# Joined loads of two head pairs, other row orders for k and v, and q turned by the crossbar for all later pairs

## The chip, the cores and the metric

The kernel runs on one core of one Trainium2 chip. The metric is the device time of one execution in microseconds (us). Engines: TensorE (PE in the profile, its weight loads PEld), VectorE (DVE), ScalarE (ACT), GpSimd (POOL) and SyncE (SP, which here only issues DMAs). Inputs are in DRAM, the output goes back there; SBUF holds 128 partitions, and TensorE writes into PSUM.

## The reference

Eight batches of eight heads, 576 rows, 64 columns a head; then a two-layer network over all 4608 rows. All in float32.

```python
scores = scale * np.matmul(q, k.transpose(0, 1, 3, 2))
thresh = np.max(scores, axis=-1, keepdims=True) - tau          # tau = 0.02
scores = np.where(scores >= thresh, scores, -1000000000.0)
scores = scores - np.max(scores, axis=-1, keepdims=True)
attn = np.exp(scores)
attn = attn / (np.sum(attn, axis=-1, keepdims=True) + 1e-09)
attn_out = np.matmul(attn, v)                                  # (8, 8, 576, 64)
x = attn_out.transpose(0, 2, 1, 3).reshape(4608, 512)
h = x @ w_in                                                   # (512, 2048)
out = (h - np.tanh(h)) @ w_out                                 # (2048, 512)
```

## The kernel before, in words

**Tiles.** The 64 heads are taken as 32 pairs, four to a batch. A pair has 2 x 576 query rows, that is nine tiles of 128 rows: four of each head, and one shared tile with the last 64 rows of both (`place`, L307). The main loop (L730) goes through 288 tiles, one a step. For one tile the work is spread over many steps: scores are made 8 steps ahead (`scores`, L313), TensorE's result is copied out by DVE, which also takes the maximum (L346); 5 steps ahead ScalarE makes z from it (`kink`, L365, L373); at its own step the exponential is taken (`weights`, L382); two steps later TensorE multiplies by v (`attend`, L414). z has to be turned between kink and weights. For pairs 0 to 5 TensorE does that; from pair 6 on, SP issues one crossbar transpose (a DMA from SBUF to SBUF) for every two tiles, `zT` (L380), and ScalarE reads zT in the exponential (L409).

**q, k and v of a pair.** `load` (L138) brings each as float32: rows 0 to 511 of both heads with four rows to a partition (L145), and the last 64 rows of both heads in a second, small DMA (L153 for q and k, where partition 2s + h takes row s of head h; L151 for v, into 64 partitions). `split` (L186) makes q and k on POOL into two fp16 parts, high and low, stored side by side. `turn` (L253) transposes them so that the 128 partitions hold 64 high and 64 low parts: on TensorE with nine transposes into PSUM (L240) and a DVE copy out (L268), or, for q of some pairs, by a crossbar transpose that SP issues (L257, `qT`). For k a copy `kS` with both halves swapped follows on POOL (L274). `split_v` (L219) copies v to bf16 on POOL. `q_by_dma` (L249) names the pairs whose q goes by the crossbar: from pair 8 on those with p % 4 != 0.

A score tile is four matmuls (L336): q against kT and against kS, each over 512 and then 64 keys. The shared tile (L327) does that for each head in one half of the array; where q was turned by the crossbar its rows alternate by head, so the weights are read with step two.

**The network.** TensorE makes h (`hidden`, L505, PSUM banks `psH`, two of them), ScalarE the tanh (L518), DVE the difference g (L524), TensorE the output (`project`, L531), DVE or ScalarE copy it out and SP stores it (L547). These steps are put between the attention's by a written pattern (L563).

**What sets the order.** Everything is issued in program order, on each engine's own in-order queue. A plan (L671 to L699) says at which step each part of a pair's preparation is issued, counted back from `first = 9 p - 8`. For the later pairs: loads of k, q, v at first - 17, - 15, - 13 for even pairs and - 16, - 14, - 12 for odd ones; splits at - 10 and - 9 (at - 8 and - 7 where TensorE turns q), k turned at - 6, v split at - 4, q turned by the crossbar at - 7 (even) or - 6 (odd), by TensorE at - 2. Within a step the order is: scores, kink and zT, tanh, weights, network, stores, attend, then the plan. So on SP a step's zT comes before the stores and loads of that step. Weights of the network come in 16 pieces during the first 54 steps (L663, L667).

Of the kernel before, what the change touches and what calls it, by code (L numbers as in the profile page):

```python
# [9 lines left out]
F32 = mybir.dt.float32  # L10
BF16 = mybir.dt.bfloat16
FP16 = mybir.dt.float16
# [6 lines left out]
def kernel(  # L19
# [11 lines left out]
    nc = tc.nc  # L31
    P = 128
# [13 lines left out]
    HPAIR = H // 2  # L46
# [85 lines left out]


    raws = {}

    def load(p, t):  # L138
        b, h0 = p // HPAIR, 2 * (p % HPAIR)
        hs = slice(h0, h0 + 2)  # L140
        src = {"k": k, "q": q, "v": v}[t]
        eng = nc.sync
        r = raws[p, t] = raw_pool.tile([P, 10, D], F32, name=f"{t}raw", tag=t)
        n = 8 if t == "v" else 10
        eng.dma_start(  # L145
            out=r[:, 0:n, :].rearrange("p (h c) d -> p h (c d)", h=2)[:, :, 0 : 4 * D],
            in_=src[b, hs, 0:512, :].rearrange("h (p c) d -> p h (c d)", c=4),
        )
        rem = src[b, hs, 512:S, :].rearrange("h s d -> s h d")
        if t == "v":  # L150
            eng.dma_start(out=r[0:64, 8:10, :], in_=rem)  # L151
        else:
            eng.dma_start(out=r[:, 4, :], in_=rem)  # L153

    def load_first(t, h, eng):

        src = {"k": k, "q": q}[t]
        if (0, t) not in raws:
            raws[0, t] = raw_pool.tile([P, 10, D], F32, name=f"{t}raw", tag=t)
        r = raws[0, t]  # L160
        if h is None:
            rem = src[0, 0:2, 512:S, :].rearrange("h s d -> s h d")
            eng.dma_start(out=r[:, 4, :], in_=rem)
        else:
            eng.dma_start(
                out=r[:, 5 * h : 5 * h + 4, :].rearrange("p c d -> p (c d)"),
                in_=src[0, h, 0:512, :].rearrange("(p c) d -> p (c d)", c=4),
            )
# [17 lines left out]
    def split(p, t):  # L186
        x = raws.pop((p, t))[:, 0:9, :]
        hl = hl_pool.tile([P, TPP, 2, D], FP16, name=f"{t}hl", tag=t)
        nc.gpsimd.tensor_scalar(
            out=x, in0=x, scalar1=QKSC, scalar2=1.0, op0=ALU.mult, op1=ALU.mult  # L190
        )
        nc.gpsimd.tensor_copy(out=hl[:, :, 0, :], in_=x)
        nc.gpsimd.tensor_tensor(  # L193
            out=hl[:, :, 1, :], in0=x, in1=hl[:, :, 0, :], op=ALU.subtract
        )
        hls[p, t] = hl
# [21 lines left out]

    def split_v(p):  # L219
        r, vb = raws.pop((p, "v")), vbs[p % NV]  # L220
        nc.gpsimd.tensor_copy(
            out=vb[:, :, 0:4, 0:D],
            in_=r[:, 0:8, :].rearrange("p (h c) d -> p h c d", h=2),
        )
        nc.gpsimd.tensor_copy(out=vb[0:64, :, 4, 0:D], in_=r[0:64, 8:10, :])
        nc.gpsimd.tensor_copy(out=vb[64:P, :, 5, 0:D], in_=r[0:64, 8:10, :])

    mats = {}  # L230


    by_head = lambda ap: ap.rearrange("p (s h) -> p h s", h=2)
    in_heads = lambda ap: ap.rearrange("p (h s) -> p h s", h=2)

    def turn_chunk(out, c, lhsT):
        rhs = ident_f16
        if c == 4:
            out, rhs = in_heads(out), by_head(rhs)
        nc.tensor.matmul(  # L240
            out=out, lhsT=lhsT, rhs=rhs, is_transpose=True, start=True, stop=True
        )
# [5 lines left out]

    def q_by_dma(p):  # L249

        return p >= 2 * HPAIR and p % 4 != 0

    def turn(p, t):  # L253
        hl = hls.pop((p, t))
        if t == "q" and q_by_dma(p):
            m = mats[p, t] = qk_pool.tile([P, W], FP16, name=f"{t}T", tag=t)
            nc.sync.dma_start_transpose(  # L257
                out=m.rearrange("p (c r) -> p c r", c=TPP),
                in_=hl.rearrange("p c a d -> p (c a d)"),
            )  # L260
            return
        ps = ps_big.tile([P, W], FP16, name=f"ps_{t}", tag="big")
        for c in range(TPP):
            turn_chunk(
                ps[:, c * P : (c + 1) * P], c, hl[:, c, :, :].rearrange("p a d -> p (a d)")
            )
        m = qk_pool.tile([P, W], FP16, name=f"{t}T", tag=t)
        nc.vector.tensor_copy(out=m, in_=ps)  # L268
        mats[p, t] = m
        if t == "k":  # L270
            sw = qk_pool.tile([P, W], FP16, name="kS", tag="ks")
            for lo, hi in ((0, D), (D, 0)):
                o, i = sw[lo : lo + D, :], m[hi : hi + D, :]
                nc.gpsimd.tensor_copy(out=o, in_=i)  # L274
            mats[p, "ks"] = sw

    def turn_first(t, part):

        hl = hls[0, t[0]]
        c0, c1 = ((0, 5), (5, TPP))[part]  # L280
        pl, tag = (ps_y, "y") if t == "ks" else (ps_h, "h")
        ps = pl.tile([P, 5 * P], FP16, name=f"ps1_{t}", tag=tag)
        for c in range(c0, c1):
            o = ps[:, (c - c0) * P : (c - c0 + 1) * P]
            if t == "ks":
                for a in range(2):
                    turn_chunk(o[64 * a : 64 * a + 64, :], c, hl[:, c, 1 - a, :])
            else:
                turn_chunk(o, c, hl[:, c, :, :].rearrange("p a d -> p (a d)"))
        if part == 0:  # L290
            mats[0, t] = qk_pool.tile([P, W], FP16, name=f"{t}T", tag=t)
        dst, n = mats[0, t][:, c0 * P : c1 * P], (c1 - c0) * P
        if part == 1 or t == "q":
            nc.scalar.copy(out=dst, in_=ps[:, 0:n])
        else:
            nc.vector.tensor_copy(out=dst, in_=ps[:, 0:n])


    MAIN = (slice(0, 512), slice(640, W))
    REM = (slice(512, 576), slice(576, 640))  # L300
    scs, mxs, nbs, zs, zts, pts, ops = {}, {}, {}, {}, {}, {}, {}

    def kind(i):
# [9 lines left out]
    def scores(i):  # L313
        p, hh, t = place(i)
        qT, kT, kS = mats[p, "q"], mats[p, "k"], mats[p, "ks"]
        ps = ps_big.tile([P, 1024], F32, name="psS", tag="big")
        main, rem, lo = slice(0, 512), slice(512, 576), 0
        if kind(i) == "B":
            main, rem, lo = slice(512, 1024), slice(448, 512), 448
        if hh is None:  # L320
            qrem = REM
            if q_by_dma(p):
                qrem = (slice(512, 640, 2), slice(513, 640, 2))
            for n, kk in enumerate((kT, kS)):
                for dst, srcs in ((main, MAIN), (rem, REM)):
                    for hh in range(2):
                        nc.tensor.matmul(  # L327
                            out=ps[64 * hh : 64 * hh + 64, dst],
                            lhsT=qT[:, qrem[hh]], rhs=kk[:, srcs[hh]],
                            start=(n == 0), stop=(n == 1),  # L330
                        )
        else:
            lhs = qT[:, (5 * hh + t) * P : (5 * hh + t + 1) * P]
            for n, kk in enumerate((kT, kS)):
                for dst, src in ((main, MAIN[hh]), (rem, REM[hh])):
                    nc.tensor.matmul(  # L336
                        out=ps[:, dst], lhsT=lhs, rhs=kk[:, src],
                        start=(n == 0), stop=(n == 1),
                    )
        sc = sc_pool.tile([P, S], F32, name="sc")  # L340
        if kind(i) == "B":
            mx = mxs[i] = mxs.pop(i - 1)
        else:
            mx = mxs[i] = mx3[i // 2 % len(mx3)]
        c = int(kind(i) == "B")
        nc.vector.tensor_scalar(  # L346
            out=sc, in0=ps[:, lo : lo + S], scalar1=SC, scalar2=None,
            op0=ALU.mult, op1=ALU.max, accum_out=mx[:, c : c + 1],
        )
        scs[i] = sc  # L350
# [163 lines left out]
    def bend():  # L514
        while halves:
            m, n, ps = halves.pop(0)
            th = t_pool.tile([P, MB], F32, name="th")
            nc.scalar.activation(out=th, in_=ps, func=ACT.Tanh)  # L518
            ths.append((m, n, ps, th))

# [8 lines left out]
    def project(m, ms, part, ps, last, cols=slice(0, d_model)):  # L529
# [4 lines left out]
            )  # L534
        if part == 3:
            nc_ = cols.stop - cols.start
            yo = y_pool.tile(
                [P, nc_], F32, name="yo", tag="yo" if nc_ == d_model else f"yo{int(last)}",
                bufs=2 if nc_ == d_model else 1,
            )  # L540
            if last:
                nc.scalar.copy(out=yo, in_=ps)
            else:
# [16 lines left out]
    EARLY = lambda m: 3 if m else 3  # L560
    LAST = 1

    PATTERN = lambda m: '-h--h-hh--h-hh-h-hh-h--hh-h--hh-y-yy' if m == 0 else 'hyhyhyhyhyhyhyhyhyhyhyhyhyhyhyhy' if m == B - 2 else 'yhyhyyy-yhyhhyyhy-hhhyhh-hyhyhy-yhhy'  # L563

    FIRST = 3
    quarters = lambda m: [(m, ms, part) for ms in range(4) for part in range(4)]
# [112 lines left out]
    )  # L679

    plan = {}
    for p in range(1, NPAIR):
        first = TPP * p - AHEAD
        for d, f in PREP[3 if p == 1 else 0 :]:
            d -= p == 1 and d == 3
# [150 lines left out]
```

## Time and profile before

| | |
|---|---|
| runs (us) | 518.08, 518.08, 518.48; median 518.08 |
| profiled execution: time, span | 518.02 us, 516.2 us |
| granted TensorE clock | 1.0 |
| busy share of the span: PE, PEld, DVE, ACT, POOL | 96%, 55%, 81%, 84%, 56% |
| DMA: bytes moved, read from and written to HBM | 86.79 MB, 36.70 MB, 9.44 MB |
| zT transposes, qT transposes issued by SP | 117, 18 |
| main loads of k, q, v (256 KB each) issued by SP | 31, 31, 32 |
| remainders of k, q, v (32 KB each) issued by SP | 31, 32, 32 |
| TensorE transposes of q (L240), copies of q by DVE (L268) | 126, 13 |

The profile is of one execution. A line of a timeline gives the start and the length in us, the engine and line, the operation, what it writes and reads, and in brackets how long the engine was idle before it and what ended that. `SPq` lines are SP's queue: the time for which the instruction held SP, not that of the transfer. A landing time counts from the start of the issue to the last byte's semaphore. "x4" on a line is several instructions shown as one, with the stretch that they cover.

### The profile page before, as it was taken

To read this page: it belongs to the slowest core of one execution; us is meant where nothing else is said; L and a number is where in the kernel's file an instruction comes from. 1 tells how busy PE (TensorE), PEld (TensorE's weight loads), DVE (VectorE), ACT (ScalarE), POOL (GpSimd) and SP (SyncE) were. 2 spreads that over 40 slices of the span, in tenths; PEclk is the share of its full clock that TensorE was granted. 3 is DMA by queue.
4 is the path that set the end of the run, shared out by engine and by line. 5 is a ranking of instruction groups with operands and counts; after the bars stand their busy time and mean duration, and the time that the engine had idled before them with its cause. 6 is when DMAs were issued, how large, how long until landed. Compare 5 with 4: busy or idle time off the path is not lost.

```text
span 516.2 us, 12626 instructions
## 1 busy us (share of the span) xinstructions
PE 497.8 (96%) x4540; PEld 285.3 (55%) x4606; DVE 418.8 (81%) x1179; ACT 432.8 (84%) x617; POOL 290.2 (56%) x390
## 2 busy tenths in 40 slices
PE   8999899889999999999999999999999999999997
PEld 4666566555555555555555555555555555544444
DVE  5999889998899988998899888998999887644440
ACT  5999999999899989998999989998999899543430
POOL 8999999776565656566666656566656620000000
PEclk9999999999999999999999999999999999999999
DMA  7852659999999999999999998999989976311013
GB/s 205 259 151 90 205 196 227 165 190 181 193 190 190 207 203 194 187 193 212 201 176 190 197 220 195 183 198 197 203 179 193 172 140 116 97 41 42 20 43 82
DMA packets 208607, 86.79 MB, mean 168 GB/s; under 512 B 176160, under 2 KB 200992, under 8 KB 208544
## 3 DMA queue, kind: packets, MB, share of 16 engines
q1 hardware_dynamic: 207952, 85.56, 80.6%
q8 instruction: 36, 0.59, 0.5%
q10 hardware_dynamic: 592, 0.43, 0.3%
q14 instruction: 27, 0.22, 0.1%
HBM read 36.70 MB, written 9.44 MB: 89 GB/s over the span
## 4 chain that ended last, share of the span: by engine, by line
PE 77%; POOL 9%; ACT 4%; DVE 3%; issue 3%; DMA 2%; SPq 1%; POOLq 0%; ACTq 0%; DVEq 0%
PE psY L531 22%; PE psH L505 19%; PE psS L336 18%; PE psO L439 5%; PE psS L327 3%; PE psHt L505 3%; PE ps_k L240 3%; POOL kS L274 2%; DMA kraw<-in_k_dram 2%; POOL w_in_sb L655 1%; PE psO L450 1%; ACT pT L409 1%; POOL khl L193 1%; PE psO L432 1%; ACT z L373 1%
## 5 line engine op out<-in xcount | busy, mean ns | idle before, releaser
L373 ACT ACTIVATE z<-sc,nb 128x576 bf16<-128x576 f32 x288 | 217.5, 770 | 23.9 <-DVE nb L358 22.2
L346 DVE TENSOR_SCALAR_CACHE_REDUCE sc<-psS 128x576 f32<-128x576 f32 x288 | 213.7, 752 | 17.5 <-PE psS L336 13.3
L531 PE MATMUL psY<-w_out_sb,g 128*128 128x512 bf16 (+1 forms) x565 | 140.2, 373 | 1.3 <-issue 0.2
L409 ACT ACTIVATE pT<-zT 128x1152 f16<-128x1152 bf16 x117 | 134.8, 1152 | 1.7 <-DMA zT<-z 1.4
L274 POOL COPY kS<-kT 64x1152 f16<-64x1152 f16 x62 | 70.7, 1141 | 110.9 <-DVE nb L358 59.6
L505 PE MATMUL psH<-xT,w_in_sb 128*128 128x512 bf16 x443 | 117.8, 379 | 3.5 <-issue 1.1
L336 PE MATMUL psS<-kT,qT 128*128 128x512 f16 (+1 forms) x512 | 104.4, 285 | 4.7 <-DVE sc L346 2.4
L336 PEld LDWEIGHTS <-qT 128*128 128x128 f16 x1024 | 72.9, 97 | 56.5 <-issue 5.5
L524 DVE SCALAR_TENSOR_TENSOR g<-th,psH 128x512 bf16<-128x512 f32 x128 | 87.5, 683 | 18.3 <-ACT th L518 18.0
L336 PE MATMUL psS<-kS,qT 128*128 128x512 f16 x496 | 101.4, 286 | 0.0
L518 ACT ACTIVATE th<-psH 128x512 f32<-128x512 f32 x128 | 74.5, 582 | 20.9 <-PE psH L505 20.9
L531 PEld LDWEIGHTS <-g 128*128 128x128 bf16 x592 | 51.1, 98 | 54.0 <-DVE g L524 0.4
L505 PEld LDWEIGHTS <-w_in_sb 128*128 128x128 bf16 x576 | 49.0, 98 | 56.3 <-issue 3.4
L439 PE MATMUL psO<-vb,pT 128*128 128x65 bf16 x1024 | 53.3, 194 | 0.0
L439 PEld LDWEIGHTS <-pT 128*128 128x128 f16 x1024 | 44.2, 98 | 9.4
L193 POOL TENSOR_TENSOR khl<-kraw,khl 128x576 f16<-128x576 f32 x31 | 39.7, 1280 | 2.6
L193 POOL TENSOR_TENSOR qhl<-qraw,qhl 128x576 f16<-128x576 f32 x31 | 39.7, 1280 | 2.6
L401 ACT ACTIVATE pT<-psZ 128x512 f16<-128x512 bf16 (+1 forms) x54 | 35.1, 654 | 2.2 <-PE psZ L392 1.8
L544 DVE COPY yo<-psY 128x512 f32<-128x512 f32 (+1 forms) x31 | 21.1, 681 | 14.7 <-PE psY L531 13.8
L465 DVE TENSOR_TENSOR osb<-psO,rc 128x256 bf16<-128x256 f32 x64 | 27.2, 424 | 2.2
L432 PE MATMUL psO<-vb,pT 128*128 128x130 bf16 x128 | 28.1, 220 | 0.1
L268 DVE COPY kT<-ps_k 128x1152 f16<-128x1152 f16 x31 | 23.4, 756 | 4.4 <-PE ps_k L240 4.3
(79 smaller groups left out, 509.7 us busy)
## 6 DMA issues: line engine op xcount, KB each, us to landing
vraw<-in_v_dram SPq DMA_DIRECT2D x32, 256.0 KB, 3.4
out_dram<-yo SPq DMA_DIRECT2D x32, 256.0 KB, 2.9
kraw<-in_k_dram SPq DMA_DIRECT2D x31, 256.0 KB, 3.3
qraw<-in_q_dram SPq DMA_DIRECT2D x31, 256.0 KB, 3.4
wt<-in_moe_w_in_dram SPq DMA_DIRECT2D x8, 512.0 KB, 4.6
wt<-in_moe_w_out_dram SPq DMA_DIRECT2D x8, 512.0 KB, 4.0
zT<-z SPq DMA_TRANSPOSE x117, 3.7
qraw<-in_q_dram SPq DMA_DIRECT2D x32, 32.0 KB, 3.1
```

Of the source, the lines that this page charges most:

```text
L193: nc.gpsimd.tensor_tensor(out=hl[:, :, 1, :], in0=x, in1=hl[:, :, 0, :], op=ALU.subtract)
L274: nc.gpsimd.tensor_copy(out=o, in_=i)
L336: nc.tensor.matmul(out=ps[:, dst], lhsT=lhs, rhs=kk[:, src], start=(n == 0), stop=(n == 1),)
L346: nc.vector.tensor_scalar(out=sc, in0=ps[:, lo : lo + S], scalar1=SC, scalar2=None, op0=ALU.mult, op1=ALU.max, accum_out=mx[:, c : c + 1],)
L373: nc.scalar.activation(out=z, in_=sc, func=ACT.Prelu, bias=nb, scale=1.0, alpha=STEEP)
L401: nc.scalar.activation(out=pt[:, off * P : (off + n) * P], in_=ps[:, 0 : n * P], func=ACT.Exp)
L409: nc.scalar.activation(out=pt[:, 0 : n * P], in_=zts.pop(i)[:, 0:n, :], func=ACT.Exp)
L439: nc.tensor.matmul(out=po[:, t - 1 + ab, :], lhsT=pt[:, blk * P : (blk + 1) * P], rhs=vb[:, hh, c, :], start=False, stop=(n == 7), skip_gr ...
L505: nc.tensor.matmul(out=ps, lhsT=w_in_sb[:, c, n * P : (n + 1) * P], rhs=xs[m][:, c, :] if m < B else xR[:, c, :, :], start=(c == 0), stop= ...
L518: nc.scalar.activation(out=th, in_=ps, func=ACT.Tanh)
L524: nc.vector.scalar_tensor_tensor(out=gs[m][:, n, :], in0=th, scalar=-1.0, in1=ps, op0=ALU.mult, op1=ALU.add,)
L531: nc.tensor.matmul(out=ps, lhsT=gs[m][:, n, ms * P : (ms + 1) * P], rhs=w_out_sb[:, n, cols], start=(n == 0), stop=(n == DF_C - 1),)
```

## The change

From pair 8 on (`DUAL = 8`, the third batch) the loads of an even pair p bring pair p + 1 too (`MM = 2`), at first - 16 (k), - 14 (q) and - 12 (v) of the even pair. A tile of raw data holds two pairs; there are still two such tiles for each of k, q and v.

k of two pairs is one DMA: partition r holds nine consecutive rows 9r to 9r + 8 of the two heads taken as one list of 1152 rows, 2304 bytes at a time. So partitions 0 to 63 belong to one head, and the keys of a head lie in runs of 64 columns of kT (`main_keys`, `rem_keys`). v follows the same order: rows 9r to 9r + 3 of a head go to partitions 0 to 63, rows 9r + 4 to 9r + 8 to partitions 64 to 127, as two DMAs. q of two pairs is one DMA of the first 512 rows as before, and one small DMA for each pair's last rows, with head 0 in partitions 0 to 63 and head 1 in 64 to 127.

q of every pair from 8 on goes by the crossbar, so pairs 8, 12, 16, 20, 24 and 28 too. For these the splits move to first - 10 and - 9, and q is turned at - 7. Per two pairs SP issues six load DMAs in place of twelve. Some lines are rewritten without another effect for pairs 0 to 7; the output buffers of the last half-width stores come from the pool of `th`.

```diff
+    DUAL = 8
+    MM = 2
+    ONACT = ''
 
     def load(p, t):
         b, h0 = p // HPAIR, 2 * (p % HPAIR)
+        src = {"k": k, "q": q, "v": v}[t]
+        eng = nc.scalar if p >= DUAL and t in ONACT else nc.sync
+        both = raw_pool.tile([P, 2, 10, D], F32, name=f"{t}raw", tag=t)
+        if p >= DUAL:
+            both = both[:, 0:MM, :, :]
+            for a in range(MM):
+                raws[p + a, t] = both[:, a, :, :]
+            rows = src[b, h0 : h0 + 2 * MM, :, :]
+            if t == "v":
+                rows = rows.rearrange("h (p c) d -> p h (c d)", c=TPP)
+                dst = both.rearrange("p a (h c) d -> p (a h) (c d)", h=2)
+                eng.dma_start(out=dst[0:64, :, 0 : 4 * D], in_=rows[:, :, 0 : 4 * D])
+                eng.dma_start(out=dst[64:P, :, :], in_=rows[:, :, 4 * D :])
+            elif t == "q":
+                eng.dma_start(
+                    out=both.rearrange("p a (h c) d -> p (a h) (c d)", h=2)[:, :, 0 : 4 * D],
+                    in_=rows[:, 0:512, :].rearrange("h (p c) d -> p h (c d)", c=4),
+                )
+                for a in range(MM):
+                    eng.dma_start(
+                        out=both[:, a, 4, :], in_=rows[2 * a : 2 * a + 2, 512:S, :]
+                    )
+            else:
+                eng.dma_start(
+                    out=both[:, :, 0:TPP, :].rearrange("p a c d -> p a (c d)"),
+                    in_=rows.rearrange("(a h) s d -> a (h s) d", h=2).rearrange(
+                        "a (p c) d -> p a (c d)", c=TPP
+                    ),
+                )
+            return
...
     def split_v(p):
         r, vb = raws.pop((p, "v")), vbs[p % NV]
+        lo = 64 if p >= DUAL else 0
...
-        nc.gpsimd.tensor_copy(out=vb[0:64, :, 4, 0:D], in_=r[0:64, 8:10, :])
-        nc.gpsimd.tensor_copy(out=vb[64:P, :, 5, 0:D], in_=r[0:64, 8:10, :])
+        nc.gpsimd.tensor_copy(out=vb[0:64, :, 4, 0:D], in_=r[lo : lo + 64, 4:10:5, :])
+        nc.gpsimd.tensor_copy(out=vb[64:P, :, 5, 0:D], in_=r[lo : lo + 64, 4:10:5, :])
...
     def q_by_dma(p):
-        return p >= 2 * HPAIR and p % 4 != 0
+        return p >= DUAL
...
+    def main_keys(p, kk, hh):
+        if p < DUAL:
+            return kk[:, MAIN[hh]]
+        return kk[:, 0 : 8 * P].rearrange("p (a n r) -> p n a r", a=2, n=4)[
+            :, :, :, 64 * hh : 64 * hh + 64
+        ]
+
+    def rem_keys(p, kk, hh):
+        return kk[:, 8 * P + 64 * hh : 8 * P + 64 * hh + 64] if p >= DUAL else kk[:, REM[hh]]
...
             qrem = REM
-            if q_by_dma(p):
-                qrem = (slice(512, 640, 2), slice(513, 640, 2))
...
+    LATER = {
+        0: (
+            ("kl", 16), ("ql", 14), ("vl", 12), ("ks", 10), ("qs", 9),
+            ("qt", 7), ("kt", 6), ("vs", 4), ("kw", 2),
+        ),
+        1: (
+            ("ks", 10), ("qs", 9), ("qt", 6), ("kt", 6), ("vs", 4),
+            ("kw", 2),
+        ),
+    }
```

In `LATER` the letters are load, split and turn of k, q, v, and the number the steps before `first`, for even and odd pairs; `kw` does nothing here.

## The prediction

> **What bounds the kernel now.** I read the chain of work that ended last first, then the busy time by stretches of 18 steps (one step of the main loop is one score tile), then the timelines of TensorE, the SP queue and ScalarE around the work that the change touches, and the landing times of the transfers.
>
> ```profile
> PE 77%; POOL 9%; ACT 4%; DVE 3%; issue 3%; DMA 2%; SPq 1%; POOLq 0%; ACTq 0%; DVEq 0%
> ```
>
> ```profile
> core 0: us, PE busy (x) PEld busy (x) DVE busy (x) ACT busy (x) POOL busy (x), PEclk, DMA share, GB/s
> ...
> 225.05:253.40 28.35, 27.98 (x255) 15.81 (x262) 24.73 (x74) 26.12 (x36) 18.05 (x24) 1.00 1.06 201
> 253.40:280.60 27.20, 26.95 (x257) 15.45 (x261) 25.23 (x71) 25.60 (x36) 16.36 (x22) 1.00 1.09 186
> ```
>
> The columns are the stretch, its length, then busy time and instructions of each engine, the granted TensorE clock, the DMA share. The reader is to see that TensorE is idle for only 0.25 to 0.37 us of some 28, at full clock, and ScalarE for 1.6 to 2.2 us. Two pairs take 55.55 / 2 = 27.8 us, a step 1.54 us. From 113 to 420 us TensorE is the bound; around 85 to 113 us it is not (24.78 busy of 28.00, DVE 25.73).
>
> **What goes from TensorE.** Pairs 8, 12, 16, 20, 24 and 28 have q turned by nine TensorE transposes and a DVE copy; these go to the crossbar. Two places of the TensorE timeline, the usual one and that of pair 8:
>
> ```profile
> 209.62 1.03 PE L505 MATMUL psH<-xT,w_in_sb 128*128 128x512 bf16 x4
> 210.49 0.67 PE L240 MATMUL ps_q<-ident_f,qhl 128*128 128x128 f16 x9
> 210.99 0.41 PE L336 MATMUL psS<-kT,qT 128*128 128x512 f16 x2
> ```
>
> ```profile
> 99.16 0.66 PE L240 MATMUL ps_q<-ident_f,qhl 128*128 128x128 f16 x9
> 100.56 0.41 PE L336 MATMUL psS<-kT,qT 128*128 128x512 f16 x2 [0.74 <-DVE sc L346]
> ```
>
> Matmuls overlap, so the price is from start to start: 210.99 - 210.49 = 0.50 us, and the same at the other four. At pair 8 TensorE then waits for DVE, so what counts is the DVE copy (L268, 0.757 us). Sum: 5 x 0.50 + 0.76 = **3.3 us saved**. The other five copies (3.8 us of DVE) and nine weight loads each are hidden behind a busier TensorE. When they go, TensorE stays the bound, since ScalarE has 25.6 of some 26.8 us then.
>
> **What the SP queue loses and gains.** SP issues nearly everything, in program order. Per 18 steps before: 9 zT transposes x 1.48 us (L380's median issue) + 1.5 qT x 1.34 + 6 main loads x 0.57 + 4 remainders (L153) x 0.56 + 2 v remainders (L151) x 0.65 + 2 stores x 0.56 = 23.3 of 27.8 us. After: 13.3 + 2 x 1.34 + six loads x 0.58 + 1.1 = 20.6. SP gets 2.7 us back, though it issues six more qT; those of pairs 8, 12, ... go out at first - 7, far from the loads. This would help, were the issue time what decides.
>
> **Where the joined loads land.** What counts for zT is the time from the end of z to the exponential (L409) that reads it. Behind v's loads, on SP and then on ScalarE:
>
> ```profile
> 193.90 1.64 SPq L380 DMA_TRANSPOSE zT<-z  x1
> 195.58 0.62 SPq L145 DMA_DIRECT2D vraw<-in_v_dram  x1
> 196.25 0.65 SPq L151 DMA_DIRECT2D vraw<-in_v_dram  x1
> 197.00 4.05 SPq L380 DMA_TRANSPOSE zT<-z  x2
> ```
>
> ```profile
> 193.63 0.76 ACT L373 ACTIVATE z<-sc,nb 128x576 bf16<-128x576 f32 x1
> ...
> 201.94 1.16 ACT L409 ACTIVATE pT<-zT 128x1152 f16<-128x1152 bf16 x1 [0.23 <-DMA zT<-z]
> ```
>
> z ends at 194.39; SP reaches its transpose at 197.00, 2.6 us late; it lands 4.9 us after that, and the exponential has waited 0.23 us. So there are 201.71 - 194.39 = **7.3 us** from z to its use, and this one spent 7.5. The run has four such waits:
>
> ```profile
> ACT pT L409 <- DMA zT<-z: 1.4, 4, 0.6
> ```
>
> The landing times (us from issue, shortest/median/longest) of zT, of the k and q remainders (L153, 32 KB; on the DRAM side 64 rows by two heads, into all 128 partitions) and of v's remainder (L151, the same 32 KB, into 64 partitions):
>
> ```profile
> L380 SPq DMA_TRANSPOSE zT<-z x117: 1242/1477/2679, 80.6 to 439.8; - x117
> ...
> DMA to landing us min/median/max: 3.2/3.7/6.4
> ```
>
> ```profile
> L153 SPq DMA_DIRECT2D kraw<-in_k_dram x31: 549/565/989, 4.4 to 398.5; - x31
> ...
> DMA to landing us min/median/max: 2.5/3.0/7.2
> ```
>
> ```profile
> L151 SPq DMA_DIRECT2D vraw<-in_v_dram x32: 635/654/1008, 3.0 to 404.8; - x32
> ...
> DMA to landing us min/median/max: 2.6/3.9/5.6
> ```
>
> The reader is to see that shape costs: with half the partitions the same bytes land 0.9 us later, and the transpose behind v needs 4.9 us against 3.7. Yet the change gives v two loads of 64 partitions each (0.59 MB in place of 0.03), and gives q two remainders a pair of pairs whose DRAM side has an outer dimension of only two heads. No row shows such a shape. Bounds: the profile's queue row (80.6% of 16 engines' 516.2 us over 207952 packets) makes a packet 0.032 us; 128 packets spread over 16 engines are 0.26 us, over one 4.1. The extra time of a remainder is thus between 0 and 3.8 us (a gain is excluded: bytes and packets are the same). I take 0.9, from the nearest row, L151 against L153. Bytes: 512 KB of weights land in 4.0 us, 256 KB in 3.4, so another pair's 288 KB adds 0.7.
>
> Now the queue, from a zT that is on time at step first - 16 (zT is due every 3.09 us; gaps of 0.06 us counted). 1.48 + k 0.57 + qT 1.34 makes the next zT 0.5 us late; + 1.48 + q's three issues 1.69 makes that of first - 12 late by 0.8. It lands in 3.7 + 0.7 + 2 x 0.9 = 6.2: 7.0 of 7.3, just in time. But its issue holds SP: over L380's rows the issue grows from 1.24 to 2.68 while the landing grows from 3.2 to 6.4, 0.45 us for each, so 1.48 + 0.45 x 2.5 = 2.6. With v's two issues (1.41 with gaps) the zT of first - 10 is 1.7 late, and lands behind v in 4.9 + 0.7 + 0.9 = 6.5. Together 8.2, so ScalarE waits 0.9 us, and 0.3 more on the mean for a store that falls between (0.6 in every second case): 1.2 us. Queued behind that exponential on ScalarE are the next z and the tanh; behind the tanh, DVE's g and the freeing of the two psH banks, which TensorE needs. The longest such wait before, 0.6 us, left no gap on TensorE, so I let 0.55 be absorbed: 0.65 us lost at each of 12 joined loads, **7.8 us**.
>
> The Trainium skill, "DMA: Bandwidth & Descriptors", section "Why a DMA increments its semaphore by 16 and not by 1", states that a transfer runs on the largest count of engines, at most 16, that divides the slowest dimension of both sides. By that rule each new q remainder has two engines with 64 packets each, an estimate of 2.05 us at the row's 0.032, 1.15 more than I take; at two a load the sum would be some 12 x 2.3 us higher, about 550 us. No row of this trace shows a transfer with so small an outer dimension.
>
> **Edits at nothing.** The keys are read as eight runs of 64 columns: two runs of 65 (L450) and one of 130 (L432) both take 220 ns in the median, equal to 1 ns a break, so at most 7 breaks x 480 matmuls x 1 ns = 3.4 us; I take 0. q's remainder rows no longer alternate by head; the weight loads of the shared tile (L327) take 106 to 115 ns in both forms. Splits of pairs 8, 12, ... move two steps earlier on POOL, which idles for 10 of 28 us; if that cover were gone, k's turn would wait. Odd pairs load nine steps earlier into buffers whose last reader ran some 20 steps before. v's copy on POOL keeps its 512 columns. The last stores' buffers come from the th ring, free by then.
>
> **Sum.** The profiled execution took 518.02 us (span 516.2, 1.8 around it), 0.06 under the median of 518.08. 518.0 - 3.3 + 7.8 = **522.5 us**.
>
> **Rivals.** *The loads stay hidden (not slower):* SP's 2.7 us back keep every zT inside 7.3 us. For it: only 1.4 us of such waits in all, and most landings near 3.7. Against: the clumping above, and a DMA share already above 1. It decides as long as a remainder costs under about 0.4 us: then 518.0 - 3.3 = 514.7. *Strided keys:* 3.4 us more on TensorE, decisive above 1 ns a break if the loads hide: 518.1, a draw. *Nothing on the path:* the freed half microsecond is taken up by another wait, such as z for DVE's nb (22.2 us in 36 waits): 518 within 1. *Remainders far worse:* nearer one engine than sixteen, at 1.9 us each: 12 x 2 us more than forecast, 546.
>
> **How the numbers follow.** Forecast case 0.44, own range 519.2 to 533; far worse 0.11; hidden loads 0.35 (513.5 to 516.8); draws 0.10. The range leaves out the far-worse case and the outer tenth: **514 to 535**. About 0.2% (1 us) is what a measurement of this kernel can tell from no change: faster 0.35, same 0.10, slower 0.55.
>
> **What would show it.** ps_q matmuls 126 to 72, qT issues 18 to 24 (the saving); the wait of pT for zT from 1.4 to some 14 us in 12 clusters behind q's and v's loads; landings of q's remainders near 4 us against 3.0; zT's issues behind them near 2.6; the 18-step stretches at 27.8 - 0.25 + 0.65 = 28.2 us. If the wait of pT stays near 1.4 us and the stretches shrink by 0.25, my queue step is wrong. If the landings of q's remainders are above 6 us, its price is.

## The result, and the profile after

The changed kernel takes **535.73 us** (median of 4 runs, 534.83 to 536.63) against 518.08 beside it: ratio 1.0339, 95% interval 1.0318 to 1.0359. It is 17.7 us slower, where 4.4 were forecast, and just outside the range. Its profiled execution has a span of 534.7 us at a granted clock of 0.997. Executions fall into a fast and a slow state, the slow one at a lower granted clock; every ratio is of fast ones alone, and only run 10 below had slow ones, two of its four, the profiled one among them.

The chain of work that ended last, by engine, and the start of its list by line:

```profile
PE 47%; ACT 14%; DMA 14%; POOL 9%; DVE 9%; issue 5%; SPq 1%; ACTq 0%; POOLq 0%
PE psY L584 16%; DMA zT<-z 12%; PE psH L558 11%; PE psS L389 9%; ACT z L426 5%; ACT pT L462 5%; ACT th L571 4%; DVE g L577 3%; DVE sc L399 3%; PE psO L492 3%; PE psHt L558 3%; POOL kS L318 2%; PE ps_k L276 1%; POOL w_in_sb L710 1%; POOL khl L224 1%
```

TensorE had 77% of this chain before, DMA 2%. Now 14% of the span go by in DMAs (12% in zT alone), and ScalarE and DVE, which stand in the same loop of z, zT, exponential, tanh and g, have 23% in place of 7%.

One stretch of the middle (start and end, length, then busy us and instructions of PE, PEld, DVE, ACT, POOL, then clock, DMA share, GB/s):

```profile
core 0: us, PE busy (x) PEld busy (x) DVE busy (x) ACT busy (x) POOL busy (x), PEclk, DMA share, GB/s
...
197.00:225.00 28.00, 25.95 (x245) 14.48 (x244) 22.32 (x64) 24.25 (x35) 17.43 (x22) 1.00 0.94 195
```

In the kernel before, TensorE was busy 27.6 to 27.8 us of each 28. Over the ten stretches from 113 to 393 us it is busy 267.6 of 280, against 276.9. ScalarE is less busy too, and single instructions take what they took (z 769 ns on the mean, 770 before): the engines wait for one another. From 113 us to the end of the stage some 307 us passed before, eleven times 27.8; the span is 18.5 us longer, so 18 steps take about 1.7 us more, where 0.4 were forecast.

The waits that grew (engine and line, what it waited for: us in total, times, longest):

```profile
DVE g L577 <- ACT th L571: 67.4, 67, 2.3
ACT pT L462 <- DMA zT<-z: 36.6, 22, 3.5
POOL qraw L220 <- DMA qraw<-in_q_dram: 24.3, 11, 2.7
```

The second line answers to "1.4, 4, 0.6" of before: the exponential waits for its transpose 22 times, nearly two for each of the twelve joined loads. The first is what is queued behind it: the tanh comes late for g (30.5 us in 36 times before, of which 30.2 fell after 421 us). The third is new: POOL waits for q at 11 of the 12 joined loads.

The SP queue at one joined load (start, us, line, transfer):

```profile
228.08 0.58 SPq L167 DMA_DIRECT2D kraw<-in_k_dram  x1
228.77 1.29 SPq L296 DMA_TRANSPOSE qT<-qhl  x1
230.15 2.70 SPq L433 DMA_TRANSPOSE zT<-z  x1
232.94 0.53 SPq L599 DMA_DIRECT2D out_dram<-yo  x1
233.53 0.42 SPq L158 DMA_DIRECT2D qraw<-in_q_dram  x1
234.00 1.14 SPq L163 DMA_DIRECT2D qraw<-in_q_dram  x2
235.24 3.02 SPq L433 DMA_TRANSPOSE zT<-z  x1
238.31 0.80 SPq L155 DMA_DIRECT2D vraw<-in_v_dram  x1
239.16 0.62 SPq L156 DMA_DIRECT2D vraw<-in_v_dram  x1
239.88 3.83 SPq L433 DMA_TRANSPOSE zT<-z  x2
```

The starts of three successive zT are 5.09 and 4.64 us apart, and they are due every 3.09. SP is never idle here. The transposes themselves hold it: 2.70 us behind k and qT, 3.02 behind q, against 1.35 in the median of all. ScalarE, at the same place:

```profile
240.86 1.16 ACT L462 ACTIVATE pT<-zT 128x1152 f16<-128x1152 bf16 x1 [1.07 <-DMA zT<-z]
241.93 1.42 ACT L426 ACTIVATE z<-sc,nb 128x576 bf16<-128x576 f32 x2
244.66 1.16 ACT L462 ACTIVATE pT<-zT 128x1152 f16<-128x1152 bf16 x1 [1.31 <-DMA zT<-z]
```

Two waits in a row, 2.4 us, with the next z's queued behind the first. Of the edits held to cost nothing, these are the groups (busy us, mean ns):

```profile
L389 PE MATMUL psS<-kS,qT 128*128 128x512 f16 (+1 forms) x512 | 104.9, 286 | 0.0
...
L276 PE MATMUL ps_q<-ident_f,qhl 128*128 128x128 f16 x72 | 5.8, 225 | 0.9 <-DVE sc L399 0.6 <-POOL qhl L224 0.3
```

The score matmuls last 286 ns as before (L336: 286): the strided keys cost nothing. The transposes of q on TensorE fell from 126 to 72, as forecast.

### The profile page after: what moved, and what is told of

The parts are those of the page before. It is cut to its first block, busy times and chain, and to the rows that moved or that the text cites. A ratio compares the mean times of both kernels' runs of the same rounds, so it can differ in the third digit from the quotient of the medians.

```text
span 534.7 us, 12469 instructions
## 1 busy us (share of the span) xinstructions
PE 505.3 (95%) x4552; PEld 282.6 (53%) x4552; DVE 413.9 (77%) x1173; ACT 432.5 (81%) x617; POOL 292.7 (55%) x390
## 4 chain that ended last, share of the span: by engine, by line
PE 47%; ACT 14%; DMA 14%; POOL 9%; DVE 9%; issue 5%; SPq 1%; ACTq 0%; POOLq 0%
PE psY L584 16%; DMA zT<-z 12%; PE psH L558 11%; PE psS L389 9%; ACT z L426 5%; ACT pT L462 5%; ACT th L571 4%; DVE g L577 3%; DVE sc L399 3%; PE psO L492 3%; PE psHt L558 3%; POOL kS L318 2%; PE ps_k L276 1%; POOL w_in_sb L710 1%; POOL khl L224 1%
## 5 line engine op out<-in xcount | busy, mean ns | idle before, releaser
L462 ACT ACTIVATE pT<-zT 128x1152 f16<-128x1152 bf16 x117 | 135.2, 1155 | 36.8 <-DMA zT<-z 36.6
L584 PE MATMUL psY<-w_out_sb,g 128*128 128x512 bf16 (+1 forms) x592 | 146.6, 375 | 0.0
L558 PE MATMUL psH<-xT,w_in_sb 128*128 128x512 bf16 x480 | 123.6, 380 | 9.0 <-DVE g L577 8.7
L389 PE MATMUL psS<-kS,qT 128*128 128x512 f16 (+1 forms) x512 | 104.9, 286 | 0.0
L220 POOL TENSOR_SCALAR qraw<-qraw 128x576 f32<-128x576 f32 x31 | 20.9, 673 | 24.3 <-DMA qraw<-in_q_dram 24.3
```

Source lines behind the costliest of these rows:

```text
L389: nc.tensor.matmul(out=ps[:, dst], lhsT=lhs, rhs=cols(p, kk, hh), start=(n == 0), stop=(n == 1),)
L462: nc.scalar.activation(out=pt[:, 0 : n * P], in_=zts.pop(i)[:, 0:n, :], func=ACT.Exp)
L558: nc.tensor.matmul(out=ps, lhsT=w_in_sb[:, c, n * P : (n + 1) * P], rhs=xs[m][:, c, :] if m < B else xR[:, c, :, :], start=(c == 0), stop= ...
L584: nc.tensor.matmul(out=ps, lhsT=gs[m][:, n, ms * P : (ms + 1) * P], rhs=w_out_sb[:, n, cols], start=(n == 0), stop=(n == DF_C - 1),)
```

## The experiments

All times are medians, each beside the kernel before (518.0 to 518.2) on the same chip. "Wait" is the total wait of the exponential for zT in the one profiled execution, with its count: 1.4 us in 4 before, 36.6 in 22 after. That execution isn't always near the median: in run 2 it is the longest (532.91 us), in run 16 the shortest (518.47). "Cluster" is the group of joined loads on SP: k at first - 16, the qT of the odd pair before at what is first - 15 of this pair, q at first - 14, v at first - 12.

**1. Only q by the crossbar.** The kernel before, with one edit:

```diff
-        return p >= 2 * HPAIR and p % 4 != 0
+        return p >= 2 * HPAIR
```

> The kernel before with one part of the change alone: q of pairs 8, 12, 16, 20, 24 and 28 goes by the crossbar too, with its splits two steps earlier; loads, row orders and key order stay as before. Theory A (the loads are the cost): the saving of the prediction comes out, 518.1 - 3.3 = 514.8 us, and the wait of the exponential for zT stays below 5 us. Theory B (six more crossbar transposes are what SP and the DMA engines can't carry): 522 us or more, with that wait above 15 us.

520.77 us, ratio 1.0048 (1.0028 to 1.0068), wait 21.9 in 21. Neither held: the time lies between the two, the wait is theory B's. TensorE loses work, but with the old loads, twelve issues per two pairs, six more qT already make zT late. This part alone costs 2.7 us.

**2. The remainder's shape.** The changed kernel, with the 64 rows outermost on both sides again (and the row order of the shared tile that goes with it):

```diff
-                        out=both[:, a, 4, :], in_=rows[2 * a : 2 * a + 2, 512:S, :]
+                        out=both[:, a, 4, :],
+                        in_=rows[2 * a : 2 * a + 2, 512:S, :].rearrange("h s d -> s h d"),
```

> The changed kernel, but q's last rows are loaded with the row as the outer dimension on the DRAM side and the heads alternating over the partitions, as before the change (64 rows by two heads in place of two heads by 64 rows), and the shared tile's weights are read with step two; all else as changed, output the same. Theory A1 (the shape of the remainders is the cost, as the prediction had it): 515 to 520 us, wait of pT for zT below 6 us. Theory A2 (the joining itself is the cost: much data at once ahead of the transposes, whatever its shape): 530 us or more, the wait still above 25 us.

529.66 us, 1.0234 (1.0199 to 1.0269), wait 33.9 in 23. Near A2, whose 530 it misses by 0.3: the shape is worth 6.1 us of the 17.7, and most stays without it.

**3. All but the joining.** The changed kernel, with every load for one pair (`MM = 1`) at the old places, first - 17, - 15, - 13 for even and - 16, - 14, - 12 for odd pairs:

```diff
-    MM = 2
+    MM = 1
```

> The changed kernel with its loads no longer joined: every pair loads its own k, q and v at the steps that the kernel before had for it, with the new row orders and the new shapes (q's remainder still two heads by 64 rows, v in two loads of 64 partitions). Output the same. Theory A1 (shape): still 525 us or more, since all the short shapes are there, though spread. Theory A2 (joining): 514 to 518 us, wait of pT for zT below 5 us.

515.92 us, 0.9959 (0.9944 to 0.9974), wait 0.3 in 1. A2 holds: all of the loss comes with the joining, and what is left is 2.1 us faster than before. It is also 4.9 us faster than run 1; the two differ in the row orders, with k in one load and no remainder, but no run takes that apart.

**4. Six q back on TensorE.** The changed kernel, with q of pairs 8, 12, ... turned by TensorE at the old steps:

```diff
-        return p >= DUAL
+        return p >= DUAL and p % 4 != 0
...
+            if p % 4 == 0:
+                d = {"ks": 8, "qs": 7, "qt": 2}.get(what, d)
```

> The changed kernel with q of pairs 8, 12, 16, 20, 24 and 28 turned by TensorE again at the steps of before; joined loads and row orders stay. Output the same. Theory A (loads): TensorE has its 3.3 us of work back and SP six transposes less, none of them near a load: 533 to 539 us, about as the changed kernel. Theory B (the transposes are too many): 518 to 523 us, wait of pT for zT back below 8 us.

533.0 us, 1.0285 (1.0268 to 1.0302), wait 32.2 in 24, at the edge of theory A: 2.7 us less than the changed kernel, so the six extra qT aren't the main cost.

**5. Single loads, and the old shape.** Runs 2 and 3 together.

> e3_unjoined with q's remainder loaded with the row as the outer dimension again (heads alternating over the partitions). Output the same. In the joined form this shape cost 6.1 us (535.7 against 529.7). If the shape costs by its place on two queues it costs spread as well: 510 to 513 us. If it cost only because the joined loads left no slack (the wait of pT for zT is 0.3 us in e3_unjoined): 515 to 516.5 us, no change.

515.64 us, 0.9959 (0.9946 to 0.9972), wait 1.1 in 2: the same as run 3 within their spreads. The shape that costs 6.1 us in the cluster costs nothing measurable when the loads are small and spread out.

**6. The whole cluster elsewhere.** The changed kernel, with k, q, v seven steps earlier, so that the qT stands ahead of k and no longer between k and q:

```diff
-            ("kl", 16), ("ql", 14), ("vl", 12), ("ks", 10), ("qs", 9),
+            ("kl", 23), ("ql", 21), ("vl", 19), ("ks", 10), ("qs", 9),
```

> The changed kernel with its joined loads seven steps earlier (first - 23, - 21, - 19), so that no qT stands between or beside them on SP; size and shape as changed, output the same. If the joined loads cost by standing next to the odd pair's qT (two transposes and the load of k within three steps): 517 to 522 us, wait of pT for zT below 10 us. If a burst of 0.59 MB ahead of any zT is enough by itself: 528 us or more, wait above 20 us.

526.01 us, 1.014 (1.0113 to 1.0166), wait 21.7 in 19. Half of the loss goes; both expectations missed. POOL has no listed wait for q any more, so POOL's late q isn't needed for the other half. Nor is it on the path in the changed kernel: between 113 and 421 us POOL has no part in the chain of work that ended last, there as here, while zT's transfers have 19.0% of that stretch in the changed kernel and nothing in the one before.

**7 to 9. One of the three loaded per pair.** The changed kernel, with one of them loaded pair by pair: k at first - 17 for even and - 16 for odd pairs, q at - 15 and - 14, or v at - 13 and - 12. The edit for q:

```diff
-    MM = 2
+    MMS = {"k": 2, "q": 2, "v": 2}
+    MMS["q"] = 1
...
+            MM = MMS[t]
...
-            ("kl", 16), ("ql", 14), ("vl", 12), ("ks", 10), ("qs", 9),
+            ("kl", 16), ("ql", 15), ("vl", 12), ("ks", 10), ("qs", 9),
...
+            ("ql", 14),
             ("ks", 10), ("qs", 9), ("qt", 6), ("kt", 6), ("vs", 4),
```

> The changed kernel with k alone loaded pair by pair (0.29 MB at first - 17 and - 16), q and v joined as changed. Output the same. If the cost is the amount of data in a row, each of the three tensors has about a third of 535.7 - 515.9 = 19.8 us: 527 to 531. If k is the one (it lands 4.25 us or more after its issue and the next zT is held 2.6 to 3.1 us): 518 to 522.

> The changed kernel with q alone loaded pair by pair (at first - 15 and - 14), k and v joined as changed. Output the same. A third of the cost: 527 to 531. If q is the one (three DMAs at once, two of them on a short outer dimension): 518 to 522. If q matters only through its remainders: 529, as e2_qrem16.

> The changed kernel with v alone loaded pair by pair (at first - 13 and - 12, 0.29 MB each in two DMAs), k and q joined as changed. Output the same. Loaded singly, q saved 15.7 us and k 6.6 of the 19.8 between the joined and the single loads. If the parts add up, nothing is left for v: 534 to 537. If any part taken out of the cluster k, qT, q, v frees the queue for the others: 527 to 532.

k: 529.14 us (1.0202 to 1.0228), wait 28.5 in 19. q: **519.98** (1.0021 to 1.0047), wait 12.7 in 13. v: 540.07 (1.0372 to 1.0466), wait 35.9 in 11. q is the load that matters most; k alone gives the third that the first theory had. Single v is slower than the change itself, which neither theory had: in its trace v's two issues follow q's three with no zT between them and are held themselves (2.36 and 1.65 us at 233.28), so the next zT starts 9.21 us after the last one, where 3.09 are due.

**10. The joined loads from another queue.** The changed kernel, with GpSimd issuing the loads from pair 8 on:

```diff
-        eng = nc.scalar if p >= DUAL and t in ONACT else nc.sync
+        eng = nc.gpsimd if p >= DUAL else nc.sync
```

> The changed kernel with its joined loads (pairs from 8 on) issued by GpSimd, so that they stand in another DMA queue than the transposes; size, shape and steps as changed, output the same. If the transposes are held because they stand behind the loads in one in-order queue: the wait of pT for zT falls below 10 us and the time to 514 to 520 us, as long as GpSimd (17 of 28 us busy) has the time to issue them. If they are held because the loads fill the 16 engines whatever the queue: 528 us or more.

577.02 to 597.27 us in four executions; the two at the higher granted clocks (577.02 at 0.982, 585.08 at 0.962) give 1.1214 (1.1124 to 1.1304). That is the second theory's side. The profiled one has a clock of 0.956, so its rows are read for their size only. The wait is 87.0 in 25. The issue times of zT (ns, shortest/median/longest) and the landings of q's remainders:

```profile
L433 SPq DMA_TRANSPOSE zT<-z x117: 1242/1327/8978, 80.8 to 515.6; - x117
```

```profile
L163 POOL DMA_DIRECT2D qraw<-in_q_dram x24: 817/840/850, 85.5 to 458.0; - x24
...
DMA to landing us min/median/max: 6.9/8.8/12.0
```

The longest, at 462.5 us, has no load ahead of it on SP for 9 us, only loads that GpSimd issued, and still holds SP for 9.0 us. So it isn't the order on SP's queue alone that holds it; something that both queues share takes part. What GpSimd's own work adds to the time is not told apart. The remainders land in 8.8 us here. The Trainium skill, "DMA: Bandwidth & Descriptors", section "Issuing engines are not separate DMA queues", says that DMAs started by different engines run on the same 16 DMA engines, and that a second issuer saves issue time only. The hold agrees with the first half; of the second no saving shows, the time is 41 to 49 us longer than the changed kernel's.

**11. Single loads from that queue.** Run 5, issued by GpSimd.

> e5_unjoined16 (single loads, remainder of q with the row outermost) with the loads of pairs from 8 on issued by GpSimd. Output the same. There is 1.1 us of wait for zT left to gain, so a queue of its own for the loads gives 513 to 516 us; if GpSimd's issues cost it time that k's swapped copy or the splits then lack, 517 us or more.

518.4 us, 1.0015 (0.9998 to 1.0033), wait 5.9 in 6. Nothing is gained: 2.8 us slower than the same loads from SP.

**12. q alone elsewhere.** The changed kernel, everything still joined:

```diff
-            ("kl", 16), ("ql", 14), ("vl", 12), ("ks", 10), ("qs", 9),
+            ("kl", 16), ("ql", 21), ("vl", 12), ("ks", 10), ("qs", 9),
```

> The changed kernel with q's joined load alone seven steps earlier (first - 21, where SP has neither a qT nor another load near), k and v joined where the change has them. Output the same. If q costs 15.7 us because it stands in the cluster of k, the odd pair's qT and v: 518 to 523 us, near e8_q_each. If q's burst costs wherever it stands: 528 us or more.

**515.88 us**, 0.9962 (0.9948 to 0.9976), 2 us below the first theory's range. One number in the plan takes away all 19.8 us by which the joined loads are slower than the single ones of run 3. Waits, and SP at k and at v of one cluster:

```profile
ACT pT L462 <- DMA zT<-z: 5.9, 9, 1.1
```

```profile
272.34 0.63 SPq L167 DMA_DIRECT2D kraw<-in_k_dram  x1
273.08 1.28 SPq L296 DMA_TRANSPOSE qT<-qhl  x1
274.45 3.09 SPq L433 DMA_TRANSPOSE zT<-z  x1
277.64 0.53 SPq L599 DMA_DIRECT2D out_dram<-yo  x1
278.26 1.32 SPq L433 DMA_TRANSPOSE zT<-z  x1
279.63 0.65 SPq L155 DMA_DIRECT2D vraw<-in_v_dram  x1
280.33 0.61 SPq L156 DMA_DIRECT2D vraw<-in_v_dram  x1
281.04 3.93 SPq L433 DMA_TRANSPOSE zT<-z  x2
```

The zT behind k and qT is still held, 3.09 us. But the next one is an ordinary 1.32: it starts 3.81 us after the first, where in the changed kernel q's three issues and a hold of 3.02 stand in its place, and nothing more builds up. The holds themselves have not gone: over the SP timelines of the eleven joined loads behind the first, the zT behind k and qT is held 2.77 us in the median (2.82 in the changed kernel), that behind q 3.18 (3.32). They only no longer follow each other. TensorE has the stage again (one stretch; it is busy 279.8 of 280 us over the ten):

```profile
197.00:225.00 28.00, 27.90 (x262) 15.50 (x262) 25.06 (x73) 26.65 (x38) 18.19 (x24) 1.00 1.08 207
```

**13. Run 12 with the old shape.** The edits of runs 2 and 12.

> The changed kernel with q's joined load at first-21 and its remainders read with the 64 rows outermost on both sides. If the shape costs only where the transfers are late already: 515.0 to 516.4 us, the same as with q moved alone (515.88) within 0.5, wait of pT for zT 4 to 7 us. If it also costs where q stands apart: 513.5 to 514.9 us, the wait below 3 us, and the fastest kernel of all.

**515.49 us**, 0.9952 (0.9938 to 0.9965), wait 3.7 in 4: the time as the first theory had it, the wait just below. With q apart the shape costs nothing measurable. It is the lowest median of all, level with runs 3, 5 and 12.

**14, 15. k or v alone elsewhere.** The changed kernel, with `("kl", 23)` in place of `("kl", 16)`, or `("vl", 19)` in place of `("vl", 12)`.

> The changed kernel, with k's joined load alone moved from first-16 to first-23; q, v and the odd pair's qT stay. Theory pile (three joined loads and a qT within four steps keep the transfers and the SP queue behind; whichever load is taken out, the rest is carried): 516 to 521 us, and the wait of pT for zT below 14 us, as with q alone moved (515.9, 5.9). Rival kq (the zT held behind k and the odd pair's qT starts the lateness, q and v only pass it on): 515 to 518, the best of the four. Rival q (q itself is what comes too late for its splits, or what is slow to land): 530 to 537, wait above 28 us.

> The changed kernel, with v's joined load alone moved from first-12 to first-19; k at first-16, the odd pair's qT and q at first-14 stay. Theory pile: 516 to 521 us, wait of pT for zT below 14 us. Rival kq: k, qT and q still follow each other, so 526 to 533, wait above 20 us. Rival q: 530 to 537, wait above 28 us.

k moved: 526.65 us (1.0127 to 1.0254), wait 27.5 in 17. v moved: 536.72 (1.0307 to 1.0395), wait 37.2 in 15. "Any of the three" falls: v's place is worth nothing, as rival q had it. k's is worth 9 us, about half, where the theories had nearly all or nothing.

**16, 17. Half of q elsewhere.** The changed kernel, with q's load split into two tasks, `m` for its main load and `r` for its two remainders; run 16 has the remainders at first - 21 and the main load at first - 14, run 17 the other way round:

```diff
-            ("kl", 16), ("ql", 14), ("vl", 12), ("ks", 10), ("qs", 9),
+            ("kl", 16), ("ml", 14), ("rl", 21), ("vl", 12), ("ks", 10), ("qs", 9),
```

> The changed kernel, with q's two remainder loads (32 KB each) moved from first-14 to first-21 and q's main load (0.52 MB) left at first-14. Theory pile, counted in bytes: nearly all of the pile stays, so 527 to 533 us (about 529.7, what the other shape of the remainder gave), wait 25 to 34 us. Theory pile, counted in issues on SP (1.15 of some 4.2 us of load issues go): 524 to 531. Rival q by its remainders (they, landing last, decide): 516 to 521, wait below 14 us.

> The changed kernel, with q's main load (0.52 MB) moved from first-14 to first-21 and its two remainder loads (32 KB each) left at first-14. Theory pile, counted in bytes: 516 to 522 us, wait of pT for zT below 14 us. Theory pile, counted in issues on SP (0.5 of some 4.2 us go, the 1.15 of the remainders stay): 528 to 534. Rival q by its remainders: 528 to 537, wait above 25 us.

Remainders moved: 521.13 us (1.0034 to 1.0087; its runs spread from 518.5 to 525.1), wait 13.3 in 12. Main load moved: 522.33 (1.005 to 1.0113), wait 23.3 in 15. Run 16 comes nearest to the rival of the remainders (516 to 521), run 17 to the pile counted in bytes (516 to 522), and the two exclude each other: either half of q, taken out, gives back 13 to 15 of the 19.8 us, though the remainders have only 64 KB of its 576 and the main load only one of its three issues. Neither bytes nor issues alone account for that: the losses don't add up.

**What the runs say together.** Read by what SP issues ahead of q, at first - 14 or, in run 6, - 21:

| ahead of q | us | run |
|---|---|---|
| joined k, then qT | 535.7 | after |
| the same, v moved away | 536.7 | 15 |
| single k one zT earlier, then qT | 529.1 | 7 |
| qT, no k | 526.7 | 14 |
| qT one zT earlier, then k | 526.0 | 6 |
| joined k, then qT, but only half of q there | 521.1, 522.3 | 16, 17 |
| (q not there) | 515.9 | 12 |

A single long hold is made up for, as run 12 shows at k and at q. Two that follow each other are not, and each thing ahead of q adds its part. So the runs show the cause to be q's place behind k and the qT; joining by itself costs nothing (515.9 with joined and with single loads).

**Left open** is what holds a transpose's issue behind a load: run 10 shows that it isn't the order of SP's queue alone, and no run tells a limit in the 16 DMA engines from one in what feeds them. The SP timelines do show which transpose it is. The first one behind joined k goes out in 1.3 us: the qT, or the zT itself in runs 6 and 14, where no qT stands there (medians 1.34 and 1.31 us). The second is held (2.82 us in the changed kernel, 2.24 in run 14). In the changed kernel it is through 4.9 us after the start of k's issue, and k has landed 4.7 us after it (medians); whether the one waits for the other was not tested.

## Why the prediction was wrong in its size

- **The mechanism was right.** Late zT behind the joined loads, then the exponential, the tanh, g and TensorE: each shows in the waits above, and run 3 ties all of it to the joining.
- **The saving on TensorE was about right.** 54 matmuls and six DVE copies went (13 copies of q to 7). The best runs are 2.1 to 2.5 us under the kernel before, against 3.3 worked out; they still have waits of their own (3.7 us for zT in run 13).
- **The step that failed is the queue's: "1.48 + k 0.57 + qT 1.34 makes the next zT 0.5 us late; + 1.48 + q's three issues".** It gave the zT behind k and qT the ordinary issue time of 1.48 us and let only q's loads hold a transpose. The timeline has 2.70 (2.58 one pair of pairs later) there, and 3.02 behind q, where 2.6 was forecast; over the eleven joined loads behind the first the medians are 2.82 and 3.32. From that zT to the next, the step has 1.48 + 1.69 and a store only on the mean, some 0.3 us over the 3.09 that are due; the trace has 2.70 + store 0.53 + q 1.56 + gaps = 5.09, 2.0 over. The next gap is 1.55 over, where 0.9 was reckoned. (At 258.62 us, with no store between, the two gaps are 4.52 and 4.32.) The zT behind v then lands in 5.2 us (median), less than the 6.5 reckoned: it is its late start that costs. The wait is then 36.6 / 12 = 3.05 us for each joined load, not 1.2.
- **Why it failed there.** In the kernel before, the zT behind qT, k's main load and k's remainder took an ordinary 1.62 us, and the step took over the median of such rows:

```profile
229.76 1.29 SPq L257 DMA_TRANSPOSE qT<-qhl  x1
231.11 0.62 SPq L145 DMA_DIRECT2D kraw<-in_k_dram  x1
231.78 0.56 SPq L153 DMA_DIRECT2D kraw<-in_k_dram  x1
232.44 1.62 SPq L380 DMA_TRANSPOSE zT<-z  x1
```

The change alters two things there. Joined k has twice the bytes, and the qT now stands behind it, so that the zT is the second transpose behind k and no longer the first. Neither alone holds it: the first behind joined k takes 1.3 us (runs 6 and 14), the second behind a single k 1.4 (medians 1.36 before, 1.37 in run 7). The step doubled the bytes for landings ("another pair's 288 KB adds 0.7") but not for the hold of that zT, and gave the new order no price.
- **What is absorbed was too small, in the other direction.** (17.7 + 3.3) / 12 = 1.75 us are lost of 3.05 waited, so 1.3 are absorbed, not 0.55. This kept the time from being even higher.
- **The price of the remainder's shape was about right on the landing, too small on the hold.** With the rows outermost, run 2 has

```profile
L163 SPq DMA_DIRECT2D qraw<-in_q_dram x24: 584/599/933, 82.8 to 405.5; - x24
DMA to landing us min/median/max: 3.4/4.1/5.5
```

in place of the 3.0 of the kernel before. For the new shape the profile prints no landing; in the packed trace these transfers post three semaphore updates where other loads post sixteen, and the last comes 4.6 us after the issue (median; 4.0 to 5.1). So the shape adds about 0.5 us to the landing, less than the 0.9 taken, and "above 6 us" didn't come. But the zT behind q is held 3.32 us in the median with the new shape and 1.76 with the old one (run 2); with q apart 3.18 and 1.88 (runs 12 and 13). That is 1.3 to 1.6 us, where 0.45 x 1.8 = 0.8 was reckoned. In time the shape cost 6.1 us where q stands behind k and qT, and nothing measurable where it stands apart.
- By the rule of the Trainium skill, "DMA: Bandwidth & Descriptors", section "Why a DMA increments its semaphore by 16 and not by 1", the prediction had worked out an estimate of 2.05 us a remainder and a time near 550. The three updates fit the rule that so small an outer dimension gets few engines; the price doesn't follow: 0.5 us on the landing, 6.1 us in the cluster (run 2), nothing measurable outside (runs 3 and 5, 12 and 13).
- **Slips in the working.** That estimate sets a whole 2.05 us against an extra of 0.9; less the 0.26 of sixteen engines it is 1.79, and the sum some 544, still far over what came. "0.45 us for each" joins the ends of two ranges that don't belong to one row: the zT with the longest issue (2.68 us) landed in 4.6 us, the one that landed in 6.4 was issued in 2.05. So no row stands behind the 2.6, and that it came within 0.7 of what was measured is partly luck. SP's terms before add up to 23.4, not 23.3.
- **The rest held.** The strided keys cost nothing, as taken, and POOL's new wait for q is not on the path (run 6). The rival "loads stay hidden" had given 514.7 and is what runs 12 and 13 nearly reach: it fails by the place of q alone.

## What to carry to other kernels

Where one in-order queue issues both bulk loads and short transfers that the next stage waits for, work out the start of each short transfer in turn, with the hold that the loads ahead of it cause, and compare its distance from the last one with what is due; a load that doubles its bytes need not keep the hold of its smaller form (the second transpose behind k: 1.4 us single, 2.8 joined). Here one long hold was made up for and two in a row were not, so put at least one undisturbed transfer between two bulk loads. Before undoing a joined load, move one of its parts in the plan: here one number was worth 19.8 us, and the joining nothing.

## What was not expected of the hardware

- A crossbar transpose from SBUF to SBUF held the issuing queue for 1.24 to 4.5 us in the changed kernel, and for up to 9.0 us in run 10, where the loads were issued from another queue. Loads and stores took 0.4 to 1.2 there, from 224 to 273 us.
- With the same joined loads the kernel took 577.0 us or more from GpSimd's queue and 535.7 from SP's; with single loads 518.4 and 515.6.
- Behind a joined load of k the first transpose went out in 1.3 us and the second was held (medians 2.82 us in the changed kernel, 2.24 in run 14).
- The granted TensorE clock was 0.94 in one stretch of the changed kernel, 141 to 169 us (1.7 us of full clock), and 1.00 in the ten others from 113 to 421 us; its mean was 0.994 and 0.996 in runs 9 and 15, which are as slow, and 1.000 in the kernel before and in runs 12 and 13. What sets this off is not shown here.
